# A channel-attention kernel: four blocks of stores before the first reload, in a fixed order

## The chip, the cores and the metric

The kernel runs on one core of one Trainium2 chip. The metric is device microseconds (us) of that core. Executions of one kernel mostly agree within 0.3 to 0.5%. A few executions fall into a slower state (2 to 4% longer); they are never compared with fast ones.

## The reference

`x` is 1 x 384 x 384 x 384 in bf16, which is 113.25 MB. All else is small.

```python
xf  = x.reshape(B, H * W, C)
gap = jnp.mean(xf, 1);  gmp = jnp.amax(xf, 1)          # pool over all pixels
h_a = relu(gap @ w1);   h_m = relu(gmp @ w1)           # w1: 384 x 96
scale = sigmoid(h_a @ w2 + h_m @ w2)                   # w2: 96 x 384
return x * scale[:, None, None, :]
```

The scale depends on every pixel, so nothing can be stored before all of `x` has been read once, and the on-chip memory holds only about a quarter of `x`. Most of `x` must be read a second time.

## The kernel before

The first pass streams `x` through six slots of on-chip memory (x_79 to x_84 in the profile). A slot holds 44 rows of 384 values for each of 128 partitions, 33,792 bytes per partition. The transfers' records show that each partition's 33,792 bytes move as one packet. When the pass ends, the last six blocks are still in the slots; 10 more rows are in `acc` and 16 in PSUM, the memory that TensorE writes to (`kept_ps`).

The second pass multiplies what is resident, stores it, and reuses each slot for one of the other 20 blocks (19 of 44 rows, one of 26). Reloads go through SyncE's queue (`nc.sync`, q1), stores through ScalarE's (`nc.scalar`, q10), multiplies are on VectorE.

```python
FIRST_STORES = ((1, 2, 3, 4, 4, 6, 8, 8, 8), (8, 8, 9, 9, 10), (10, 12, 22))
FIRST_READS = (2, 2)
LEAD = 2
# ... first pass, the two-layer network, scale_bc: cut ...
    def put(block, pieces, acc_at=None):
        first, n, s = block
        j = 0
        for i, m in enumerate(pieces):
            if i == acc_at:
                put_acc()
            rows = slots[s][:, j:j + m, :]
            multiply(rows, rows)
            nc.scalar.dma_start(out=rows_of(orr, first, n)[:, j:j + m, :], in_=rows)
            j += m
    # ... cut ...
    order = blocks[n_stream:]                                   # the six resident blocks
    again = sorted(blocks[:n_stream], key=lambda b: -b[1])      # those to reload
    # read_into(s): reload the next block of `again` into slot s and append it to `order`
    k = 0
    while k < len(order):
        put(order[k], stores.pop(0) if stores else (order[k][1],), None if k else ACC_STORES_AT)
        k += 1
        if k == LEAD:
            read_into(order[k - 1][2])
            for j in range(k - 1):
                read_into(order[j][2])
        elif k > LEAD:
            read_into(order[k - 1][2])
    # ... then kept_ps: multiply into a free slot and store ...
```

`LEAD` is the number of blocks whose stores are written down before the first reload. In program order the second slot is reloaded first. The scheduler that places SyncE's instructions changed that: the kernel before in fact issues the reload of x_79 first, in two halves, at 289.6 us, and then that of x_80.

## Time and profile before

The median is 743.33 us of three runs (742.74 to 744.27). The page of the profiled run has these lines. The second and third divide the span into 40 slices of 18.5 us: busy tenths of the 16 DMA engines, and what they moved. The last two give packets, MB and the share of 16 engines' time for the reads (q1) and the stores (q10).

```profile
span 741.1 us, 2455 instructions
DMA  9999999999999969999999999999999999999998
GB/s 382 434 428 432 433 430 432 419 428 428 426 429 417 421 241 355 422 430 450 436 414 436 438 438 436 436 425 425 438 438 436 436 436 416 436 438 445 423 438 369
q1 hardware_dynamic: 10880, 199.12, 63.1%
q10 hardware_dynamic: 6192, 113.25, 35.7%
```

DMA is busy in all but the few microseconds between the passes, which is slice 15. The kernel is bound by transfers.

Three stretches of the second pass, by start and end; the columns are length, the busy time and instruction count of each engine in turn (PE and PEld are TensorE's multiplications and weight loads, DVE is VectorE, ACT ScalarE, POOL GpSimd), the granted clock of TensorE, the DMA share, and GB/s:

```profile
core 0: us, PE busy (x) PEld busy (x) DVE busy (x) ACT busy (x) POOL busy (x), PEclk, DMA share, GB/s
289.00:300.00 11.00, 0.00 (x0) 0.00 (x0) 11.00 (x7) 0.00 (x0) 0.00 (x0) 0.50 1.00 366
300.00:340.00 40.00, 0.00 (x0) 0.00 (x0) 40.00 (x7) 0.00 (x0) 0.00 (x0) 0.50 1.02 435
340.00:690.00 350.00, 0.00 (x0) 0.00 (x0) 163.88 (x19) 0.00 (x0) 0.00 (x0) 0.50 1.00 433
```

The first line is the only visible loss: 366 GB/s although the engines never rest. There the first reload starts beside small stores. The last line is the steady state at 433 GB/s, with VectorE busy less than half of the time.

How long a whole-block transfer takes from its issue to its landing, in us, is the last number of a line of the page's list of issues. Reads land after 27.4 us, stores after 74.6 us, so the backlog is in the store queue:

```profile
x_82<-in_x_dram SPq DMA_DIRECT2D x5, 4224.0 KB, 27.4
...
out_dram<-x_82 ACTq DMA_DIRECT2D x4, 4224.0 KB, 74.6
```

Last, two lines of the timeline of the steady state (start, duration, engine, line, operation).

```profile
471.31 0.33 SPq L235 DMA_DIRECT2D x_82<-in_x_dram  x1
...
478.78 8.96 DVE L206 TENSOR_TENSOR x_81<-x_81,scale_bc 128x16896 bf16<-128x16896 bf16 x1 [11.01 <-DMA x_81<-in_x_dram]
```

### The profile page before, as it was taken

Reading aid. Unit: us, or ns where it says so; the run is one execution under the profiler, and the core shown is the slowest. Engines: PE = TensorE matmul, PEld = TensorE weight load, DVE = VectorE, ACT = ScalarE, POOL = GpSimd, SP = SyncE. Lnnn points to the kernel's source line nnn. Section 1 sums busy time; section 2 is a strip of 40 time slices with the busy share of each in tenths; the row PEclk is TensorE's granted clock in tenths of the full one; section 3 lists DMA queues with packets and bytes.
Section 4 is the critical chain, followed back from the end, with each engine's and each line's share of the span. In section 5 each row is a group of like instructions: output and inputs, shape, how many; then the busy total and the mean of one; then the engine's idle time right before and its main releaser. Section 6 shows DMA issues by size and latency. Waiting matters only on the chain.

```text
span 741.1 us, 2455 instructions
## 1 busy us (share of the span) xinstructions
PE 125.8 (17%) x970; PEld 40.5 (5%) x970; DVE 488.4 (66%) x162; ACT 3.3 (0%) x9; POOL 0.7 (0%) x6
## 2 busy tenths in 40 slices
PE   3345443445445550000000000000000000000000
PEld 0011111111111130000000000000000000000000
DVE  6789999999999989999444444444444444444500
ACT  0000000000000000000000000000000000000000
POOL 0000000000000000000000000000000000000000
PEclk9665666665555555555555555555555555555555
DMA  9999999999999969999999999999999999999998
GB/s 382 434 428 432 433 430 432 419 428 428 426 429 417 421 241 355 422 430 450 436 414 436 438 438 436 436 425 425 438 438 436 436 436 416 436 438 445 423 438 369
DMA packets 17083, 312.52 MB, mean 422 GB/s; under 512 B 2256, under 2 KB 2608, under 8 KB 4912
## 3 DMA queue, kind: packets, MB, share of 16 engines
q1 hardware_dynamic: 10880, 199.12, 63.1%
q10 hardware_dynamic: 6192, 113.25, 35.7%
q8 instruction: 7, 0.11, 0.1%
q14 instruction: 4, 0.03, 0.0%
HBM read 199.11 MB, written 113.25 MB: 421 GB/s over the span
## 4 chain that ended last, share of the span: by engine, by line
another core or an unknown queue 40%; DVE 35%; DMA 16%; issue 1%; DVEq 1%; SPq 1%; PE 0%; ACT 0%; ACTq 0%
DVE acc L171 29%; DMA out_dram<-x_83 6%; DMA x_81<-in_x_dram 6%; DMA x_79<-in_x_dram 4%; DVE x_79 L206 1%; DVE x_80 L206 1%; DVE x_81 L206 1%; DVE x_83 L206 1%; DVEq L289 1%; DVE x_82 L206 1%; SPq L235 1%; DVE acc L187 0%; DVE acc L206 0%; DVE acc L167 0%
## 5 line engine op out<-in xcount | busy, mean ns | idle before, releaser
L206 DVE TENSOR_TENSOR x_80<-x_80,scale_bc 128x16896 bf16<-128x16896 bf16 (+3 forms) x9 | 45.1, 5043 | 33.0 <-DMA x_80<-in_x_dram 33.0
L206 DVE TENSOR_TENSOR x_79<-x_79,scale_bc 128x3072 bf16<-128x3072 bf16 (+7 forms) x13 | 41.8, 3261 | 30.2 <-DMA x_79<-in_x_dram 29.0
L206 DVE TENSOR_TENSOR x_83<-x_83,scale_bc 128x16896 bf16<-128x16896 bf16 x4 | 35.8, 8956 | 33.2 <-DMA x_83<-in_x_dram 33.2
L206 DVE TENSOR_TENSOR x_84<-x_84,scale_bc 128x16896 bf16<-128x16896 bf16 x4 | 35.8, 8956 | 33.1 <-DMA x_84<-in_x_dram 33.1
L206 DVE TENSOR_TENSOR x_82<-x_82,scale_bc 128x16896 bf16<-128x16896 bf16 x4 | 35.8, 8957 | 32.9 <-DMA x_82<-in_x_dram 32.9
L206 DVE TENSOR_TENSOR x_81<-x_81,scale_bc 128x16896 bf16<-128x16896 bf16 (+3 forms) x6 | 36.0, 6022 | 29.4 <-DMA x_81<-in_x_dram 29.4
L171 DVE TENSOR_TENSOR acc<-acc,x_84 128x4224 bf16<-128x4224 bf16 x20 | 47.2, 2358 | 5.9 <-DMA x_84<-in_x_dram 5.3
L132 PEld LDWEIGHTS <-small 128*1 128x1 bf16 x885 | 35.7, 111 | 228.9 <-issue 225.8
L171 DVE TENSOR_TENSOR acc<-acc,x_83 128x4224 bf16<-128x4224 bf16 (+1 forms) x19 | 43.4, 2285 | 2.1 <-DMA x_83<-in_x_dram 1.6
L171 DVE TENSOR_TENSOR acc<-acc,x_80 128x4224 bf16<-128x4224 bf16 (+1 forms) x17 | 39.9, 2347 | 3.0 <-DMA x_80<-in_x_dram 2.4
L171 DVE TENSOR_TENSOR acc<-acc,x_79 128x4224 bf16<-128x4224 bf16 (+1 forms) x17 | 38.9, 2287 | 1.5 <-DMA x_79<-in_x_dram 1.0
L171 DVE TENSOR_TENSOR acc<-acc,x_81 128x4224 bf16<-128x4224 bf16 x16 | 37.7, 2358 | 1.9 <-DMA x_81<-in_x_dram 1.4
L171 DVE TENSOR_TENSOR acc<-acc,x_82 128x4224 bf16<-128x4224 bf16 x16 | 37.7, 2358 | 1.0 <-DMA x_82<-in_x_dram 0.5
L132 PE MATMUL bank_a<-x_83,small 128*1 128x512 bf16 (+2 forms) x159 | 21.7, 575 | 25.5 <-DMA x_83<-in_x_dram 25.5
L132 PE MATMUL bank_a<-x_84,small 128*1 128x512 bf16 (+2 forms) x153 | 20.4, 571 | 26.3 <-DMA x_84<-in_x_dram 26.3
L132 PE MATMUL bank_a<-x_80,small 128*1 128x512 bf16 (+1 forms) x147 | 20.3, 588 | 24.7 <-DMA x_80<-in_x_dram 24.7
L132 PE MATMUL bank_a<-x_82,small 128*1 128x512 bf16 (+2 forms) x138 | 19.7, 595 | 20.9 <-DMA x_82<-in_x_dram 20.9
L132 PE MATMUL bank_a<-x_79,small 128*1 128x512 bf16 (+1 forms) x150 | 18.1, 526 | 28.4 <-DMA x_79<-in_x_dram 28.4
L132 PE MATMUL bank_a<-x_81,small 128*1 128x512 bf16 (+2 forms) x138 | 19.5, 592 | 19.8 <-DMA x_81<-in_x_dram 19.7
L167 DVE COPY acc<-x_79 128x4224 bf16<-128x4224 bf16 x1 | 1.3, 1261 | 5.4 <-DMA x_79<-in_x_dram 5.4
L173 DVE COPY kept_ps<-x_79 128x3072 uint32<-128x3072 uint32 x1 | 3.4, 3355 | 0.0
L206 DVE TENSOR_TENSOR x_81<-kept_ps,scale_bc 128x6144 bf16<-128x6144 bf16 x1 | 3.4, 3351 | 0.0
(37 smaller groups left out, 22.6 us busy)
## 6 DMA issues: line engine op xcount, KB each, us to landing
x_84<-in_x_dram SPq DMA_DIRECT2D x6, 4224.0 KB, 27.5
x_80<-in_x_dram SPq DMA_DIRECT2D x5, 4224.0 KB, 27.4
x_81<-in_x_dram SPq DMA_DIRECT2D x5, 4224.0 KB, 27.4
x_82<-in_x_dram SPq DMA_DIRECT2D x5, 4224.0 KB, 27.4
x_83<-in_x_dram SPq DMA_DIRECT2D x5, 4224.0 KB, 27.6
x_79<-in_x_dram SPq DMA_DIRECT2D x4, 4224.0 KB, 27.4
out_dram<-x_82 ACTq DMA_DIRECT2D x4, 4224.0 KB, 74.6
out_dram<-x_83 ACTq DMA_DIRECT2D x4, 4224.0 KB, 71.4
```

What stands on the lines that cost most here:

```text
L132: nc.tensor.matmul(sum_ps[q * QP:q * QP + 1, 0:g * P], lhsT=ones_bf[:, 0:1], rhs=rows[:, k:k + g, q * P:(q + 1) * P], start=(done + k == 0 ...
L167: nc.vector.tensor_copy(out=acc, in_=rows[:, 0:A, :])
L171: nc.vector.tensor_tensor(out=acc[:, 0:k, :], in0=acc[:, 0:k, :], in1=rows[:, j:j + k, :], op=ALU.max)
L173: nc.vector.tensor_copy(out=kept_ps.bitcast(U32), in_=rows.bitcast(U32))
L206: nc.vector.tensor_tensor(out=dst, in0=src, in1=scale_bc.unsqueeze(1).to_broadcast([P, n, C]), op=ALU.mult)
L235: nc.sync.dma_start(out=slots[s][:, j:j + m, :], in_=rows_of(xr, first, n)[:, j:j + m, :])
L289: with _tile.TileContext(nc) as tc:
```

## The change

The intent is to open the second pass with stores alone, so that no reload collides with small store pieces. The third, fourth and fifth block are now stored in pieces that grow to 24 rows, which lets the store queue be fed until the first slots are free. Then reloads start, as whole blocks. A manual schedule for SyncE makes program order binding: x_82, x_79, x_80, x_81, and so on.

```diff
-FIRST_STORES = ((1, 2, 3, 4, 4, 6, 8, 8, 8), (8, 8, 9, 9, 10), (10, 12, 22))
-FIRST_READS = (2, 2)
-LEAD = 2
+FIRST_STORES = ((1, 2, 3, 4, 4, 6, 8, 8, 8), (8, 8, 9, 9, 10), (10, 11, 11, 12), (13, 15, 16), (20, 24))
+LEAD = 4
 ... (cut() and get() removed: a reload is one whole transfer now) ...
+    in_order = ctx.enter_context(ExitStack())
+    in_order.enter_context(tc.manual_schedule(engines={mybir.EngineType.SP}))
     k = 0
     while k < len(order):
         ... (unchanged)
+    in_order.close()
```

More of the change, by code (lines that the diff above doesn't have):

```diff
@@ L226, in put @@
         assert j == n
-    def cut(n, parts):
-        return [n // parts + (k < n % parts) for k in range(parts)]
-    def get(block, pieces):
-        first, n, s = block
-        j = 0
-        for m in pieces:
-            nc.sync.dma_start(out=slots[s][:, j:j + m, :], in_=rows_of(xr, first, n)[:, j:j + m, :])
-            j += m
     order = blocks[n_stream:]
     again = sorted(blocks[:n_stream], key=lambda b: -b[1])
-    stores, reads = list(FIRST_STORES), list(FIRST_READS)
+    stores = list(FIRST_STORES)
     def read_into(s):
@@ L247, in read_into @@
             again.remove(b)
-            b = (b[0], b[1], s)
-            get(b, cut(b[1], reads.pop(0) if reads else 1))
-            order.append(b)
+            first, n, _ = b
+            nc.sync.dma_start(out=slots[s][:, 0:n, :], in_=rows_of(xr, first, n))
+            order.append((first, n, s))
+    in_order = ctx.enter_context(ExitStack())
+    in_order.enter_context(tc.manual_schedule(engines={mybir.EngineType.SP}))
     k = 0
```

## The prediction

> **What bounds it now.** The DMA engines do. The page's DMA row is 9 in 38 of 40 slices, and the queue table shows 312.5 MB at a mean of 422 GB/s. VectorE is busy 66%, and in the second pass waits only for transfers. The view of stretches gives 433 GB/s at DMA share 1.00 from 340 to 690 us; 366 GB/s at share 1.00 from 289 to 300. The second pass must move about 198 MB whatever the order. At 433 GB/s this is 457 us of the 464 us from the first multiply (277 us) to the end (741). So order can recover at most 7 us, mostly out of reach: 1.4 us before the first store moves bytes, 1.5 us after the last packet, and small packets.
>
> **Packets.** In the packet records 33,792 B takes 1.251 us and 3,072 B takes 0.122 us, so a packet costs about 9 ns beside its bytes (estimate: line through the two). Hence 403 to 412 GB/s while small stores run (281 to 290 us). It stays: the first 14 store pieces are unchanged.
>
> **The one visible loss.** The first reload (first half of x_79, issued at 289.6) starts while 6 KB stores drain. From 291 to 296 its packets and the stores beside them take up to twice their usual time: 6,144 B takes 0.455 instead of 0.234 us. Summed over packets and divided by 16 engines, this excess is about 1.5 us from 288 to 300. Reloads restarting at 314 show no excess.
>
> **What the change does.**
> - Removes: reloads at 289.6; the two halved reads (two DMAs less). The first reload is now x_82, after its stores land, about 321 us; x_79, x_80 and x_81 are free by then and follow at once.
> - Adds four store pieces: net two DMAs, 256 packets of 9 ns on 16 engines, +0.15 us.
> - Moves: stores run alone from 279 to about 321. VectorE makes 44 rows in 9.1 us, the DMA needs 10, so its lead grows from 2.8 us after x_79 to about 6 us after x_82; every piece (20 rows: 4.1 us plus 1 us to start) fits. I expect no idle gap. Later the backlog lies in the read queue instead of the store queue: the median reload takes about 60 us to land instead of 20, the median whole-block store about 45 to 60 instead of 75.
> - The last saved multiply moves before the last four blocks and waits for a store of x_80; VectorE has slack (9 of every 20 us busy) and stores stay queued, so no effect.
> - Last reload lands at about 712 instead of 694 us; the store-only tail shrinks as the opening grew.
>
> The Trainium skill, "DMA: Bandwidth & Descriptors", Queues, rings and completion order, says that each engine alternates between queues packet by packet; the trace agrees (33.8 KB both sides: equal shares; 16.9 KB reads beside 8 KB stores: 285 to 145 GB/s). So mixing adds no bandwidth.
>
> **Prediction.** Saved: about 1 us of the 1.5 us collision (some may recur at 321). Added: 0.15 us. 742.4 us, 740.3 to 744.2. Faster by over 2%: 0.01; same: 0.98; slower: 0.01.
>
> **Right if:** 366 GB/s in the slice around 290 to 300 becomes about 410 to 425; store-only until about 321; 433 GB/s afterwards; no slice between 280 and 735 under DMA 9. **Wrong if:** VectorE falls behind the stores (idle DMA between 290 and 321), the collision recurs in full with 33.8 KB reads, or deep reads starve the stores near the end.

## The result, and the profile after

The changed kernel took a median of 750.84 us in three runs, 749.49, 750.84 and 751.48. A fourth run of 780.32 us was slow and is left out. The kernel before, timed beside it, had a median of 743.8 us (742.74 to 744.9). The ratio is 1.0091, with a 95% interval of 1.0065 to 1.0117. Ratios here and below are the mean time of one kernel's fast runs over that of the other's fast runs of the same rounds, so they are not quite the ratio of the quoted medians. All ratios in this text lie within 2% of 1; the intervals say which of these small differences are clear of noise. The change is within 2%, as predicted, but it costs about 7 us where 1 us was to be saved, and it lies well outside the predicted range.

The same lines of the page after:

```profile
span 749.7 us, 2462 instructions
DMA  9999999999999959999999999999999999999997
GB/s 377 433 432 433 430 433 430 422 426 426 427 428 416 420 211 411 423 405 425 433 427 433 427 431 427 420 433 424 420 424 429 416 435 416 429 422 431 431 426 333
q1 hardware_dynamic: 10592, 199.12, 63.0%
q10 hardware_dynamic: 6768, 113.25, 35.5%
```

The DMA row looks the same, and the bytes are the same. There are 576 more store packets and 288 fewer read packets (288 more in all). From slice 19 on the rate is lower nearly everywhere. The same stretches, with one more that is used later:

```profile
core 0: us, PE busy (x) PEld busy (x) DVE busy (x) ACT busy (x) POOL busy (x), PEclk, DMA share, GB/s
289.00:300.00 11.00, 0.00 (x0) 0.00 (x0) 11.00 (x7) 0.00 (x0) 0.00 (x0) 0.50 1.02 417
300.00:340.00 40.00, 0.00 (x0) 0.00 (x0) 34.28 (x10) 0.00 (x0) 0.00 (x0) 0.50 1.01 412
305.00:320.00 15.00, 0.00 (x0) 0.00 (x0) 15.00 (x6) 0.00 (x0) 0.00 (x0) 0.50 1.02 427
340.00:690.00 350.00, 0.00 (x0) 0.00 (x0) 155.56 (x18) 0.00 (x0) 0.00 (x0) 0.50 1.00 427
```

The opening improved as meant (366 to 417 GB/s), but the stretch after it fell from 435 to 412, and the long steady stretch from 433 to 427 at the same share of 1.00. The engines do not wait; they take longer for the same bytes.

```profile
x_82<-in_x_dram SPq DMA_DIRECT2D x6, 4224.0 KB, 62.2
...
out_dram<-x_82 ACTq DMA_DIRECT2D x4, 4224.0 KB, 33.6
```

The backlog has moved from the stores to the reads, as intended. The last saved multiply (from PSUM) now waits for a store, but it delays nothing that the engines needed:

```profile
L205 DVE TENSOR_TENSOR x_80<-kept_ps,scale_bc 128x6144 bf16<-128x6144 bf16 x1 | 3.4, 3358 | 14.5 <-DMA out_dram<-x_80 14.5
```

### Where the time went

The trace records the packets of all 16 engines, each with its start, end and bytes. An undisturbed packet takes 9.1 ns plus 0.03675 ns per byte (the line through 0.122 us for 3,072 B and 1.251 us for 33,792 B). I call what a packet takes beyond this its excess, and sum it over the engines and divide by 16. The last store packet ended at 739.65 us before and at 748.45 us after. The 8.80 us between them (of these two profiled runs; the medians lie 7.0 us apart) divide so:

| term | before | after | difference, us |
|---|---|---|---|
| start of the first store | | | +0.16 |
| 9.1 ns for each packet | 5.32 | 5.49 | +0.16 |
| excess in the opening (277 to 345 us) | 1.75 | 2.39 | +0.64 |
| excess in the steady state (after 345 us) | 0.02 | 5.54 | +5.52 |
| last engine to end, less the mean engine | 0.48 | 2.64 | +2.16 |
| rest | | | +0.16 |

So there are two losses. Packets became slow in the steady state: of the 5.54 us, 5.04 are reads. From 400 to 600 us no read of 33,792 B took over 1.3 us before (0 of 1,280); after, 201 of 1,257 did, and their mean went from 1.251 to 1.295 us. Stores hardly changed (1.251 to 1.254 us). Of the 201 slow reads, 197 are among the first four of the eight rows that an engine moves of a block. And the slow packets did not hit all engines equally: at the last store the earliest and the latest engine lay 4.60 us apart, against 0.67 before, and the kernel ends with the latest.

### A number that the timeline shows: the distance

The two queues alternate row by row on each engine, so in the steady state one read row and one store row take 2 x 1.251 = 2.5 us. Each engine has 8 rows of each block, so on each queue a block ends every 20 us. What is left free is how far the end of a store block lies from the end of a read block. I call the end of the store minus the end of the read the distance, taken on the median engine. It comes mostly in steps of 2.5 us, it is only meaningful within a period of 20 us (+10 and -10 are the same), and in these two kernels the opening sets it: it is -7.5 through the whole steady state before, and 2.5 to 3.0 after.

The profile shows it without any packet records. VectorE starts its multiply when a read has landed on all engines, and SyncE issues the next reload when a store has landed on all engines. Before, SyncE's issue is at 471.31 and the multiply at 478.78: the store ended 7.5 us ahead of the read, a distance of -7.5. After:

```profile
447.01 8.96 DVE L205 TENSOR_TENSOR x_84<-x_84,scale_bc 128x16896 bf16<-128x16896 bf16 x1 [11.78 <-DMA x_84<-in_x_dram]
449.77 0.33 SPq L238 DMA_DIRECT2D x_81<-in_x_dram  x1
```

The store ends 2.8 us behind the read, and on the median engine 2.5. A rougher form of this idea (theory B: block ends within some 3 us of each other are bad) stood beside others before the first experiment. It took the experiments to find which distance matters.

### The profile page after: what moved, and what is told of

Its sections match the earlier page's. It is cut to its first block, busy times and chain, and to the rows that moved or that the text cites. A ratio compares the mean times of both kernels' runs of the same rounds, so it can differ in the third digit from the quotient of the medians.

```text
span 749.7 us, 2462 instructions
## 1 busy us (share of the span) xinstructions
PE 126.5 (17%) x970; PEld 40.8 (5%) x970; DVE 488.8 (65%) x166; ACT 3.3 (0%) x9; POOL 0.7 (0%) x6
## 4 chain that ended last, share of the span: by engine, by line
DVE 53%; another core or an unknown queue 25%; DMA 17%; issue 1%; PE 0%; SPq 0%; ACT 0%; DVEq 0%; ACTq 0%
DVE acc L170 28%; DMA x_79<-in_x_dram 6%; DMA x_81<-in_x_dram 6%; DVE x_82 L205 5%; DMA out_dram<-x_80 5%; DVE x_79 L205 4%; DVE x_80 L205 4%; DVE x_81 L205 4%; DVE x_84 L205 4%; DVE x_83 L205 4%; DMA out_dram<-x_82 1%; DVE acc L186 0%; DVE acc L205 0%; DVE acc L166 0%
## 5 line engine op out<-in xcount | busy, mean ns | idle before, releaser
L205 DVE TENSOR_TENSOR x_82<-x_82,scale_bc 128x16896 bf16<-128x16896 bf16 (+3 forms) x7 | 44.9, 6441 | 39.6 <-DMA x_82<-in_x_dram 39.6
L205 DVE TENSOR_TENSOR x_79<-x_79,scale_bc 128x3072 bf16<-128x3072 bf16 (+7 forms) x13 | 41.8, 3262 | 41.6 <-DMA x_79<-in_x_dram 40.5
L205 DVE TENSOR_TENSOR x_81<-x_81,scale_bc 128x16896 bf16<-128x16896 bf16 (+3 forms) x7 | 36.0, 5183 | 35.1 <-DMA x_81<-in_x_dram 35.1
L205 DVE TENSOR_TENSOR x_80<-x_80,scale_bc 128x16896 bf16<-128x16896 bf16 (+3 forms) x8 | 36.1, 4554 | 33.0 <-DMA x_80<-in_x_dram 33.0
L205 DVE TENSOR_TENSOR x_84<-x_84,scale_bc 128x16896 bf16<-128x16896 bf16 x4 | 35.8, 8956 | 28.6 <-DMA x_84<-in_x_dram 28.6
L205 DVE TENSOR_TENSOR x_83<-x_83,scale_bc 128x16896 bf16<-128x16896 bf16 (+2 forms) x5 | 35.9, 7194 | 22.7 <-DMA x_83<-in_x_dram 22.7
L205 DVE TENSOR_TENSOR x_80<-kept_ps,scale_bc 128x6144 bf16<-128x6144 bf16 x1 | 3.4, 3358 | 14.5 <-DMA out_dram<-x_80 14.5
## 6 DMA issues: line engine op xcount, KB each, us to landing
x_82<-in_x_dram SPq DMA_DIRECT2D x6, 4224.0 KB, 62.2
out_dram<-x_84 ACTq DMA_DIRECT2D x4, 4224.0 KB, 33.6
out_dram<-x_82 ACTq DMA_DIRECT2D x4, 4224.0 KB, 33.6
```

The lines of the kernel that those rows point to most:

```text
L205: nc.vector.tensor_tensor(out=dst, in0=src, in1=scale_bc.unsqueeze(1).to_broadcast([P, n, C]), op=ALU.mult)
```

## The experiments

Eighteen kernels ran, on five chips, each next to the kernel before on the same chip. The theories in their course: the reads are slow because the read queue is deep (62 us); because the late opening or the fixed order as such is bad; because all engines read and write in lockstep; because VectorE and the transfers meet in on-chip memory; or because of the position of read blocks against store blocks, the distance. The table at the end of this section gathers all numbers.

"Excess" in what was measured is that after 345 us, reads and stores together; "slow reads" are whole-block read packets of over 1.3 us from 400 to 600 us.

### First call: order, LEAD and depth

**Before, with SyncE's program order made binding.** The reload of x_80 then goes first.

```diff
+    in_order = ctx.enter_context(ExitStack())
+    in_order.enter_context(tc.manual_schedule(engines={mybir.EngineType.SP}))
     ... loop unchanged ...
+    in_order.close()
```

> The kernel before with one part of the change alone: the reloads stand in the program's order (x_80 before x_79), the rest as before. All theories of the slow reads expect the steady stretch as before: no whole-block read packet over 1.3 us, 433 GB/s from 400 to 600 us, reads about 27 us to landing, 742 to 745 us. If the fixed order itself were the cause, it would be near 750 us.

Measured: 748.56 us (745.56 to 753.1), ratio 1.0077 [1.0037, 1.0117]. The distance was -7.4, drifting to -6.2, with 51 slow reads of 1,276, an excess of 2.22 us, and engines 5.24 us apart at the end. Order alone cost about 5 us here, but with another picture than after: the engines were already 5 to 9 us apart in the opening, and stood at all distances between -10 and 10, so that the median says little.

**After, with LEAD 2.**

```diff
-LEAD = 4
+LEAD = 2
```

> The changed kernel with reloads beginning after two blocks again (LEAD 2), its store pieces and fixed order kept. Theory A (several queued reads are the cost) and theory B (the ends of a read block and a store block fall within some 3 us of each other) both expect the read queue to be shallow again (about 27 us to landing) and 742 to 745 us if the ends fall apart; under B it is slow if they happen to fall together. If the late opening is harmless and the store pieces are the cause, it stays near 750 us.

Measured: 747.07 us (745.68 to 752.7), ratio 1.0066 [1.0027, 1.0105]. The profile is of the slowest run (752.7): engines up to 14 us apart, a distance that slid from 9.3 to 5.0, 69 slow reads of 1,270, excess 2.32 us. An early reload does not by itself cure it.

**After, with a read queue one deep.** A one-element copy on GpSimd makes each reload wait until the one before has landed. It is written into the slot to be reloaded, so it is free of races.

```diff
+    reads = []
 def read_into(s): ...
+            if len(reads) >= 1:
+                nc.gpsimd.tensor_copy(out=slots[s][0:1, 0:1, 0:1], in_=slots[reads[-1]][0:1, 0:1, 0:1])
+            reads.append(s)
```

> The changed kernel with the late opening kept, but each reload waits until the reload before it has landed (GpSimd copies one element from the slot just read into the slot to be read; the reload overwrites it). One read in flight at a time. Theory A expects slow read packets gone (mean of whole-block read packets 1.25 instead of 1.29 us from 400 to 600 us), the spread of the 16 engines at the last store near 0.7 instead of 4.6 us, and 742 to 745 us if stores stay queued. Theory C (the pairing of the block read with the block stored beside it, which stays one or two blocks apart) expects the slow packets to stay and about 750 us.

Measured: 749.62 us (748.92 to 751.53), ratio 1.0095 [1.0078, 1.0112]. Reads landed after 22.2 us instead of 62, so the queue was shallow, and the kernel stayed as slow: 79 slow reads of 1,263, excess 4.28 us. So a deep queue is not needed for the loss. The distance changed too: it alternated between 6.2 and 11.2. (That depth alone does no harm is shown by two kernels below that are as deep and have hardly any slow reads: the old pieces, and the pieces 28 and 16.)

**After, with the 26-row block reloaded first.** This shifts all later blocks against each other.

```diff
-    again = sorted(blocks[:n_stream], key=lambda b: -b[1])
+    again = sorted(blocks[:n_stream], key=lambda b: b[1])
```

> The changed kernel with the short block of 26 rows reloaded first instead of last. Read depth stays at 3 to 4 queued (60 to 78 us to landing), but the ends of read blocks move by some 8 us against the ends of store blocks. Theory A expects the slow packets and about 750 us as in the changed kernel. Theory B expects them gone: 433 GB/s from 400 to 600 us and 743 to 746 us.

Measured: 744.37 us (743.8 to 746.89), ratio 1.0022 [1.0003, 1.0041]. The distance is 0.3; slow reads fell to 56 of 1,269, but 141 store packets were slow; excess 2.69 us. The profile is of the slowest run (746.89; the other three took 743.8 to 744.38). A change that does nothing but shift one queue by 18 rows per partition took back most of the loss. This pointed to the distance.

### Second call: shift the phase, and the parts of the change alone

**Before, with an extra read of 40 partitions.** With SyncE's order written out as it really was (that part of the edit is cut), one unneeded read into the dead `acc` is added in mid-loop. It delays the read queue on the engines that carry it.

```diff
     k += 1
+        if k == 8:
+            nc.sync.dma_start(out=acc[0:40, :, :], in_=xr[0:40 * A, :].rearrange("(p n) c -> p n c", n=A))
```

> The kernel before (its reload order written out by hand, same order), with one extra small read of 40 partitions x 8,448 B into a tile that is no longer used, issued in the steady stretch at about 410 us. Forty partitions are expected on 10 of the 16 DMA engines, 4 packets of some 0.32 us each, so 10 engines fall about 1.3 us (half a read-write pair) behind the other 6. Theory L (the kernel before is fast because its 16 engines stay in step, all reading and then all writing, and a mixed phase makes packets slow) expects slow whole-block packets after that point, hundreds over 1.28 us instead of none, and 746 to 751 us. If step does not matter, the cost is the read itself and the skew, 0.8 to 1.3 us: about 744 us and no slow packets.

Measured: 745.62 us (744.38 to 751.22), ratio 1.0041 [1.0002, 1.008]. The Trainium skill, "DMA: Bandwidth & Descriptors", Why a DMA increments its semaphore by 16 and not by 1, says that a transfer is spread over the largest number of engines up to 16 that divides its partitions, so 40 partitions go to 10 engines. The records agree: 10 engines show this read. Those 10 moved to distance 0, the other 6 stayed at -7.5, and there was 1 slow read of 1,250. Engines out of step with each other were harmless at these two distances, and so is lockstep: in the kernel before all 16 have the same distance, with no slow reads. The profile is of the fastest of the four runs; the run of 751.22 us has no trace, so what made it slow is not known.

**The same with 64 partitions,** which go to all 16 engines.

> Control of the run before: the same extra read with 64 partitions, so that all 16 engines get the same 4 small packets and stay in step. Theory L and its rival both expect about 1.3 us more than the kernel before, 744 to 745 us, and no slow packets in the steady stretch.

Measured: 745.39 us, ratio 1.0022 [1.0007, 1.0037]. The distance was near 10 at first and 0.0 afterwards; 3 slow reads of 1,245, excess 0.16 us.

**Before, with the new store pieces only.** `FIRST_STORES` of the changed kernel, all else as before.

```diff
-FIRST_STORES = ((1, 2, 3, 4, 4, 6, 8, 8, 8), (8, 8, 9, 9, 10), (10, 12, 22))
+FIRST_STORES = ((1, 2, 3, 4, 4, 6, 8, 8, 8), (8, 8, 9, 9, 10), (10, 11, 11, 12), (13, 15, 16), (20, 24))
```

> The kernel before with the new store pieces alone; reloads start at 289 us in two halves as before, in the scheduler's order. If the pieces are not the cause: 743 to 744 us, engines in step, no slow packets after 345 us. If the pieces by themselves put the engines out of step: slow packets and 745 to 750 us.

Measured: 745.68 us (744.9 to 749.14), ratio 1.0036 [1.0011, 1.0061]; distance -10, 1 slow read of 1,280, excess 0.43 us, engines 3.66 us apart. The pieces without the late start cost about 2 us, little of it (0.4 us) through slow packets in the steady state.

**After, without the manual schedule.**

```diff
-    in_order = ctx.enter_context(ExitStack())
-    in_order.enter_context(tc.manual_schedule(engines={mybir.EngineType.SP}))
     ...
-    in_order.close()
```

> The changed kernel without the fixed order of the reloads: the scheduler then puts the reload of x_79 as early as its stores allow, at about 290 us, and so takes away the late opening as well. Theory L expects the time to follow the step of the engines: near 743 us if they stay in step, 746 to 751 us if not; the queue depth should be near that of the kernel before (reads about 27 us to landing).

Measured: 747.11 us, ratio 1.0045 [1.0029, 1.0062]. The scheduler again moved the first reload early; reads landed after 28.6 us, the distance was 9.7, 10 slow reads of 1,279, excess 1.34 us, engines 5.39 us apart.

### Third call: a late opening that is fast, VectorE, the moment of issue

**After, with LEAD 3.** Three blocks of stores, then reloads; order fixed.

```diff
-LEAD = 4
+LEAD = 3
```

> The changed kernel with reloads beginning after three blocks instead of four. The stores should be some 50 us behind instead of 34 (two blocks: 80), so it lies between. If the slow packets grow as the stores come closer to the reads (theory D: the shallow store queue is the cost), the time should lie between 747 and 751 us and the excess of read packets after 345 us between 2 and 5 us per engine. If it is chance alignment of the engines, it can come out anywhere from 744 to 752 us, with a spread of several us between executions.

Measured: 743.49 us (743.35 to 743.59), ratio 0.9988 [0.9967, 1.0009]. The distance is -10, no slow read of 1,280, excess 0.00, engines 0.63 us apart. The stretches view of this kernel:

```profile
340.00:690.00 350.00, 0.00 (x0) 0.00 (x0) 147.34 (x18) 0.00 (x0) 0.00 (x0) 0.50 1.00 433
```

It is back at 433 GB/s. A late opening in a fixed order is thus not slow as such. This is the best variant found, and it can't be told from the kernel before.

**After, with VectorE nearly idle.** Reloaded blocks are multiplied in one row of 44 only, so the result is wrong (relative error 0.857).

```diff
-            multiply(rows, rows)
+            part = rows[:, 0:1, :] if k >= NS else rows
+            multiply(part, part)
```

> The changed kernel with a wrong result on purpose: of each reloaded block only one row in 44 is multiplied, so VectorE is idle for nearly all of the steady stretch; all transfers stay. If VectorE's reads and writes of the on-chip memory slow the transfers, the slow read packets (201 of 1,257 over 1.3 us from 400 to 600 us) go away and the time falls to about 743 to 745 us. If they are a matter of the transfers among themselves, they stay: over 100 slow ones and 748 us or more. Stores are issued 9 us earlier, so they are a little deeper.

Measured: 750.18 us, ratio 1.008 [1.0057, 1.0104]; distance 2.5, 162 slow reads of 1,257, excess 5.09 us. The stretches view:

```profile
340.00:690.00 350.00, 0.00 (x0) 0.00 (x0) 9.35 (x18) 0.00 (x0) 0.00 (x0) 0.50 1.00 427
```

VectorE's busy time fell from 155.56 to 9.35 us and the rate stayed at 427. VectorE's work is not what makes the packets slow.

**After, with a read queue two deep.** As the kernel with a queue one deep, but each reload waits for the one two before it (`reads[-2]`). This moves the moments at which SyncE issues from the end of a store block to the end of a read block, which at this distance is 2.7 us earlier (447.1 us instead of 449.8 in the block around 450 us), and leaves the distance.

> The changed kernel with each reload issued when the reload two before it has landed: never more than two in the read queue, never an empty one, and the moment of issue moves from the end of a store block to the end of a read block. Theory T (reads in flight while the next reload is issued are the slow ones: in the changed kernel those 10 per cent of the reads carry 1.88 of 4.77 us) expects the slow cluster to move with the issue. Theory D (shallow store queue) expects slow packets and 748 to 752 us, the clusters still at the end of store blocks. If the deep read queue were the cost, 744 us or less.

Measured: one fast run of 751.31 us, and three slow (770 to 772), so there is no ratio. In the fast run's profile reads landed after 40.5 us, the distance was 2.5, 156 slow reads of 1,259, excess 5.22 us; the slow reads still came around the ends of store blocks. So they do not follow the moment of issue, as far as a shift of 2.7 us can tell.

**After, with the old store pieces.** `FIRST_STORES` of the kernel before.

```diff
-FIRST_STORES = (..., (10, 11, 11, 12), (13, 15, 16), (20, 24))
+FIRST_STORES = (..., (10, 12, 22))
```

> The changed kernel with the store pieces of the kernel before (x_82 and x_83 whole, x_81 ends with 22 rows), the late opening and the fixed order kept. VectorE needs 9 us for the whole x_82 and its lead over the stores is only some 5 us there, so I expect the DMA engines to stand idle some 3 to 5 us between 305 and 320 us (no such gap in the changed kernel), and the time at 752 to 757 us.

Measured: 747.28 us (747.03 to 747.68), ratio 1.0041 [1.0015, 1.0067]. Slower than this was expected, since the slow packets were thought to come with the late opening; they did not. The distance is -7.4, 3 slow reads of 1,282, excess 0.05 us. Two stretches:

```profile
305.00:320.00 15.00, 0.00 (x0) 0.00 (x0) 15.00 (x3) 0.00 (x0) 0.00 (x0) 0.50 0.81 341
340.00:690.00 350.00, 0.00 (x0) 0.00 (x0) 155.65 (x18) 0.00 (x0) 0.00 (x0) 0.50 1.00 433
```

The first line shows what the smaller pieces are for: with whole blocks the DMA engines go idle (share 0.81, where the changed kernel has 1.02 at the same time), because a store cannot start until 44 rows are multiplied. The second line shows the steady state at 433. Here reads took 68.4 us and stores 24.3 us to land, so neither deep reads nor a short store queue make packets slow.

### Fourth call: set the distance on purpose

By now the theory was that a distance of 2.5 us is bad. The next four runs set it, with everything else nearly equal.

**After, with the last pieces 28 and 16 instead of 20 and 24.** The number of rows is the same; only the point changes at which x_83's store is cut in two.

```diff
-FIRST_STORES = (..., (20, 24))
+FIRST_STORES = (..., (28, 16))
```

> The changed kernel with x_83 stored as 28 and 16 rows instead of 20 and 24; nothing else differs. When the reloads begin (about 328 us) some 2.5 of the 8 packets per engine of the first piece should be left instead of less than one, so the stores' block ends should fall some 7.5 us after the reads' ones instead of 2.5. Theory B (this distance decides) expects no slow packets in the steady stretch, 433 GB/s, a spread of the engines at the last store under 2 us, and 743 to 745 us. If the distance is only a symptom: slow packets and 749 to 752 us as in the changed kernel.

Measured: 744.16 us (743.8 to 745.25), ratio 1.0017 [1.0003, 1.0032]. The distance became 5.0 (about 7.5 was expected). No slow read of 1,286, excess 0.00, engines 0.77 us apart. The stretches view, then the timeline:

```profile
340.00:690.00 350.00, 0.00 (x0) 0.00 (x0) 162.47 (x19) 0.00 (x0) 0.00 (x0) 0.50 1.00 433
```

```profile
443.52 8.96 DVE L205 TENSOR_TENSOR x<-x,scale_bc 128x16896 bf16<-128x16896 bf16 x1 [10.93 <-DMA x<-in_x_dram]
...
449.92 0.33 SPq L238 DMA_DIRECT2D x<-in_x_dram  x1
```

The issue now lies 6.4 us behind the multiply, where it was 2.8. Reads take 62.2 us and stores 37.3 us to land, as in the changed kernel. The loss fell from 0.9% to 0.2% through a change of two piece sizes that removes no work.

**The same with 16 and 28.**

> The same with 16 and 28 rows: the first piece is over before the reloads begin, so the stores' block ends should fall some 2.5 us ahead of the reads' ones (or a whole block pair later). Theory B in its first wording (ends within 3 us either way are bad) expects slow packets and 748 to 752 us; if only a store end 2.5 us behind a read end is bad, 743 to 745 us.

Measured: 750.42 us, ratio 1.0094 [1.0078, 1.0111]. The distance was expected to move to the other side, to -2.5, but it stayed at 2.5, and so did the loss: 167 slow reads of 1,260, excess 5.32 us.

```profile
340.00:690.00 350.00, 0.00 (x0) 0.00 (x0) 155.56 (x18) 0.00 (x0) 0.00 (x0) 0.50 1.00 427
```

```profile
446.82 8.96 DVE L205 TENSOR_TENSOR x<-x,scale_bc 128x16896 bf16<-128x16896 bf16 x1 [11.13 <-DMA x<-in_x_dram]
...
449.83 0.33 SPq L238 DMA_DIRECT2D x<-in_x_dram  x1
```

The edit missed the distance that it aimed at, but as a pair the two runs are what was wanted: two splits of the same 44 rows, the same multiply work, one at 5.0 us with 433 GB/s, one at 2.5 us with 427 GB/s.

**After, with an extra read of 64 partitions right behind the first reload.**

```diff
         if k == LEAD:
             read_into(order[k - 1][2])
+            nc.sync.dma_start(out=acc[0:64, :, :], in_=xr[0:64 * A, :].rearrange("(p n) c -> p n c", n=A))
```

> The changed kernel with the small extra read of 64 partitions (4 packets on each of 16 engines) put behind the first reload. It shifts reads against stores by 4 or 5 packet pairs, so the distance should become about -7.5 or -10 us. In the kernel before, the same read cost about 2 us. Theory B expects the slow packets gone and 744 to 747 us, faster than the changed kernel though it moves more bytes. If the distance does not matter: 750 to 754 us.

Measured: 744.75 us, ratio 1.0024 [1.0009, 1.0039]; distance -7.4 first and then -5.1, 4 slow reads of 1,291, excess 0.38 us. The stretches view:

```profile
360.00:690.00 330.00, 0.00 (x0) 0.00 (x0) 148.04 (x18) 0.00 (x0) 0.00 (x0) 0.50 1.00 433
```

The kernel moves more bytes than the changed one and is about 6 us faster.

**The same with 128 partitions.** It was to come round to 2.5 and be slow.

> Control for the run before: the extra read has 128 partitions, 8 packets per engine, so the shift is a whole block (8 pairs, perhaps 9) and the distance should come back to about 2.5 us (or 0). Theory B expects slow packets as in the changed kernel and 750 to 754 us if the distance is 2.5 us; if it comes out at another value, it is read as another point of the same curve.

Measured: 751.3 us (749.57 to 754.2), ratio 1.0115 [1.0088, 1.0142]. It was slow, but not for the stated reason: the distance was 5.6 to 6.8, the engines came apart in the course of the loop (the ends of a read block lay 0.7 us apart at the first reload and 8 to 10 us at the end), 74 slow reads of 1,277, excess 2.71 us. This run does not support the theory. With engines far apart, the distance of the median engine does not describe them all.

### Fifth call: make the kernel before slow

**Before, with an extra read of 48 partitions in mid-loop,** in the way of the 40 and 64 above. (The expectation has a slip: "740 to 745 GB/s" cannot be a rate; the sentence means the clean rate of about 433 GB/s.)

> The kernel before with the extra small read of 48 partitions (3 packets of 8,448 B on each of 16 engines) at about 430 us. Four such packets moved the distance of the block ends from -7.5 to 0 us, that is by 12.5 us or 5 packet pairs; three should move it by 4 pairs, from -7.5 to about 2.5 us. Theory B expects slow read packets from then on, 740 to 745 GB/s replaced by a fall of the rate from 433 to 427-430 GB/s after 450 us, a spread of the engines at the last store of 3 us or more, and 747 to 751 us. If the distance is not the cause: 744 to 745.5 us as with 64 partitions.

Measured: fast runs of 747.81 and 750.81 us (two more slow, 765.27 and 770.59), ratio 1.0071 [1.0037, 1.0105]. The extra read moved the distance from -7.5 to 2.5 inside one execution. The timeline before and after the extra read:

```profile
432.13 0.33 SPq L235 DMA_DIRECT2D x<-in_x_dram  x1
439.60 8.96 DVE L206 TENSOR_TENSOR x<-x,scale_bc 128x16896 bf16<-128x16896 bf16 x1 [10.99 <-DMA x<-in_x_dram]
...
465.67 8.96 DVE L206 TENSOR_TENSOR x<-x,scale_bc 128x16896 bf16<-128x16896 bf16 x1 [17.11 <-DMA x<-in_x_dram]
468.07 0.33 SPq L235 DMA_DIRECT2D x<-in_x_dram  x1
```

The issue leads the multiply by 7.5 us in the first pair and trails it by 2.4 us in the second. The rates of the two stretches:

```profile
340.00:420.00 80.00, 0.00 (x0) 0.00 (x0) 39.53 (x6) 0.00 (x0) 0.00 (x0) 0.50 1.01 436
450.00:690.00 240.00, 0.00 (x0) 0.00 (x0) 98.55 (x11) 0.00 (x0) 0.00 (x0) 0.50 1.00 426
```

The same kernel, on the same chip, in one execution, is clean until its phase is moved to 2.5 us, and slow from there on: 1 slow read of 377 from 400 to 465 us, and 114 of 860 from 465 to 600 us. The 40 partitions, with the same edit and no engine at 2.5, had none of 864 in the latter stretch.

**The same with 32 partitions.** A distance of 5 was expected, and with it a clean run.

> The same with 32 partitions, 2 packets per engine: about 3 pairs, from -7.5 to 5 us, the distance at which the changed kernel with 28 and 16 rows had no slow packets. Theory B expects none here and 743.5 to 745 us. If the opening comes out at another distance than -7.5 us (it did in one run with 64 partitions), the distance measured after the extra read decides, not the number of partitions.

Measured: 748.79 us (743.54 to 749.21), ratio 1.0042 [1.0000, 1.0084]. The distance went from -10 to 2.5, not 5, and the packets were slow from then on: 119 slow reads of 1,256, excess 3.71 us, 426 GB/s from 450 to 690 us. The aim was missed, and the rule held at the distance that the run really had. One of its four runs (743.54) was as fast as the kernel before; it has no trace, so whether its distance differed is not known.

### All runs

Distance in us on the median engine; excess in us after 345 us; spread in us between the first and the last engine at the last store; median of the fast runs in us. All but the last two columns are of the one profiled execution, which with LEAD 2, with the short block first and with 128 partitions was the slowest of its kernel.

| kernel | distance | slow reads | excess | spread | median | ratio |
|---|---|---|---|---|---|---|
| before | -7.5 | 0/1280 | 0.02 | 0.67 | 743.8 | |
| after | 2.5 | 201/1257 | 5.54 | 4.60 | 750.84 | 1.0091 |
| before, order fixed | -7.4 to -6.2 | 51/1276 | 2.22 | 5.24 | 748.56 | 1.0077 |
| after, LEAD 2 | 9.3 to 5.0 | 69/1270 | 2.32 | 8.83 | 747.07 | 1.0066 |
| after, reads one deep | 6.2 / 11.2 | 79/1263 | 4.28 | 1.15 | 749.62 | 1.0095 |
| after, short block first | 0.3 | 56/1269 | 2.69 | 2.32 | 744.37 | 1.0022 |
| before, +40 partitions | 0 and -7.5 | 1/1250 | 0.01 | 1.69 | 745.62 | 1.0041 |
| before, +64 partitions | 0.0 | 3/1245 | 0.16 | 2.32 | 745.39 | 1.0022 |
| before, new pieces | -10 | 1/1280 | 0.43 | 3.66 | 745.68 | 1.0036 |
| after, order free | 9.7 | 10/1279 | 1.34 | 5.39 | 747.11 | 1.0045 |
| after, LEAD 3 | -10 | 0/1280 | 0.00 | 0.63 | 743.49 | 0.9988 |
| after, no multiply | 2.5 | 162/1257 | 5.09 | 5.36 | 750.18 | 1.0080 |
| after, reads two deep | 2.5 | 156/1259 | 5.22 | 5.46 | 751.31 (one run) | none |
| after, old pieces | -7.4 | 3/1282 | 0.05 | 0.55 | 747.28 | 1.0041 |
| after, (28, 16) | 5.0 | 0/1286 | 0.00 | 0.77 | 744.16 | 1.0017 |
| after, (16, 28) | 2.5 | 167/1260 | 5.32 | 4.68 | 750.42 | 1.0094 |
| after, +64 partitions | -5.1 | 4/1291 | 0.38 | 1.28 | 744.75 | 1.0024 |
| after, +128 partitions | 5.6 to 6.8 | 74/1277 | 2.71 | 7.95 | 751.3 | 1.0115 |
| before, +48 partitions | -7.5, then 2.5 | 115/1237 | 3.67 | 4.74 | 749.3 (two runs) | 1.0071 |
| before, +32 partitions | -10, then 2.5 | 119/1256 | 3.71 | 3.66 | 748.79 | 1.0042 |

Every kernel with a distance of 2.5 us, six of six, had over a hundred slow reads. Every kernel whose engines ended within 1.3 us of each other at -10, -7.5, -5 or +5 us had fewer than five.

Engine by engine the rule holds in some of the other kernels too. The records kept do not name the engine, but a packet starts where the packet before it on its engine ends, so an engine's packets can be followed (not quite surely where several end at once). With the short block first, 55 of the 56 slow reads are on engines whose own distance is 2.5 (of some 460 reads there), and 1 of 768 is on engines at 0. With the order fixed in the kernel before, 26 of 159 reads at 2.5 were slow, and with 128 partitions 24 of 150: about the share of the changed kernel, 194 of 1,212. But with 128 partitions 50 of 1,098 reads on engines at 5.0 and 7.5 were slow too, where the pieces 28 and 16 had none of 1,173 at 5.0. And with the short block first 124 of 734 stores were slow on engines at 0, where the kernel before with 64 partitions had 4 of 911.

## Why the prediction was wrong

**What was right.** The opening without reloads ran at 417 GB/s instead of 366. There was no idle gap: from 305 to 320 us the DMA share is 1.02. The extra packets cost 0.16 us, as predicted. Whole-block reads took about 60 us to land. The multiply from PSUM waited 14.5 us and cost nothing.

**The step that failed: "433 GB/s afterwards", from "So mixing adds no bandwidth".** The argument took a packet's time to depend on its size alone, because 1,280 of 1,280 reads in the kernel before did so. That holds at some distances, among them the one at which that kernel happens to run, but not at all of them. The changed kernel runs at 2.5 us, where the same 33,792 bytes take 1.295 us on average instead of 1.251. The rate was 427 GB/s, and slow packets cost 5.5 us. This is the largest part of the 8.8 us.

**A cost that was not in the sum at all: engines that come apart.** The kernel ends with the last of 16 engines. That term was 0.48 us before and 2.64 after, another 2.2 us. The prediction's sum treats the engines as one, which was nearly true of the kernel before.

**A term with the wrong sign: the collision.** The prediction saved about 1 us of the excess at 291 to 296 us, and said that "some may recur". It recurred in full: 1.50 us from 290 to 300 us before, 1.51 us from 325 to 335 us after, where the reloads begin (first read packet at 328.9 us) and the rate of 300 to 340 us is 412 GB/s. The packets were larger than before, so the small stores were not the reason. About half of it or more lies in stores that moved in the last 3 us before the first read packet (0.73 us before, 0.94 after), when no reload was moving yet; what slows them there is not known. The rest of the growth from 1.75 to 2.39 us, 0.57 us, is in stores that run alone from 290 to 325 us: they moved 427 GB/s (the stretch from 305 to 320 us), not 433.

**Smaller misses.** Stores alone lasted until about 328 us, not 321 (the first reload was issued at 324.2 us). The last reload landed at 721 us, not 712; in the clean variant with pieces (28, 16) it landed at 712.3, so this miss follows from the slow packets. Whole-block stores took 33.6 us to land, not 45 to 60.

**What is shown and what is open.** It is shown that the loss in the steady state follows the distance: two splits of one block give 433 GB/s at 5.0 us and 427 at 2.5; an extra read takes the changed kernel from 2.5 to -5.1 and makes it faster; an extra read takes the kernel before from -7.5 to 2.5 and makes it slow within one execution. It is shown that VectorE's work and a deep queue are not the cause, that the slow reads do not move with the issue when that moves by 2.7 us, and that a late opening in a fixed order need not be slow (LEAD 3). The fixed order alone did cost about 5 us in the kernel before, with its engines apart. It is not shown why 2.5 us is bad. At that distance the engines start a new read block about one row pair before a new store block, and a pattern of memory addresses could be behind it, but no run separates that. The distance is also not the whole law: with the queue one deep, with the short block first, with the order fixed in the kernel before, and with LEAD 2 or 128 extra partitions, a smaller number of packets was slow at other distances. In all of these the engines were 1 to 14 us apart from each other in the steady state, so no one distance describes them; taken engine by engine, 2.5 us accounts for the slow reads with the short block first, and for only a part of them with the order fixed and with 128 partitions. With the queue one deep (engines 2 to 4 us apart, 1.15 at the last store, distances of 6.2 and 11.2 us in turn) and with LEAD 2 no reason is known.

## What to carry to other kernels

When two full queues share the DMA engines, compare GB/s at a DMA share of 1.00 between kernels and look at the duration of single packets: a busy share of 1.00 hides slow packets, and it hides that one engine ends later than the others. Here the opening set how the read blocks lay against the store blocks in the rest of the loop, so a change to the opening must be judged by the steady state that it leaves behind, and one that should be neutral is worth trying with two or three other piece sizes or leads before it is dropped. Here LEAD 3, or pieces of 28 and 16, gave back what the change had lost (743.49 and 744.16 us against 750.84), but neither beat the kernel before: with the engines at 433 GB/s there was hardly anything left to win.

## What the Trainium skill lacked or had wrong

- "DMA: Bandwidth & Descriptors", Queues, rings and completion order, describes how an engine takes turns between queues, but no page says that a packet's time depends on how the blocks of two full queues lie against each other. The runs show 1.295 instead of 1.251 us for a mean read packet of 33,792 B, and 427 instead of 433 GB/s, at a distance of 2.5 us, and none of it at 5.0, -5.1, -7.5 or -10 us.
- The same section says that an engine drains a whole packet, typically 9 to 17 descriptors, before it switches. That section does not say how many bytes this is. In these traces the records of the two queues alternate one 33,792 B row at a time, which gives the 2.5 us step of the distance; how many descriptors such a record holds they do not show, so they neither confirm nor contradict the count.
- No page has a number for the cost of engines that come apart. Between the first and the last of 16 engines lay 0.67 us at the last store before and 4.60 us after, and the last engine ended 0.48 and 2.64 us later than the mean one.
- "DMA: Bandwidth & Descriptors", Where 436 GB/s comes from, says that for transfers between HBM and on-chip memory the HBM side of about 358 GB/s binds. The core alone, reading and writing at once, held 433 GB/s for 350 us, right at the 435 GB/s that the same section gives for the fabric. "HBM Reference" puts a core that streams alone at about 425 GB/s, which is closer.
- "DMA: Bandwidth & Descriptors", Measured, gives about 10.5 ns per packet, a floor of 0.67 us divided by 64 packets, for transfers issued from GpSimd. Here, with transfers issued from SyncE and ScalarE, the part of a packet on one engine beside its bytes is about 9.1 ns, an estimate from 0.122 us for 3,072 B and 1.251 us for 33,792 B; records of 4 B take 9 ns. The two need not be the same quantity.
